# Block-sparse attention and a gated feed-forward layer on one core: the loads of the second batch lose their gate, one early key load goes to another queue, and the order of all engines is written anew

## The chip, the core and the metric

The kernel runs on one core of one Trainium2 chip. The core has five engines with a queue of instructions each: TensorE (PE in the profile, its weight loads PEld) multiplies matrices, VectorE (DVE) and ScalarE (ACT) work element by element, GpSimd (POOL) does so too and issues some transfers, and SyncE (SP) only issues transfers. Each engine takes its instructions in the order in which they are written; between engines semaphores make one wait for another. Transfers run on 16 DMA engines. The metric is the device time of one execution in microseconds (us), the median of several runs; less is better.

## The reference

```python
scores = scale * np.matmul(q, k.transpose(0, 1, 3, 2))    # q, k, v: 4 batches, 8 heads, 768 positions, 64
mask = |blk_i - blk_j| <= 1, first and last block row and column, 3 sampled blocks per row   # blocks of 32
attn = softmax(np.where(mask, scores, -1e9))
x = np.matmul(attn, v) -> (3072, 512)                     # heads side by side
h = x @ w_in                                              # 512 x 2048
out = (h * (1.0 / (1.0 + np.exp(-beta * h)))) @ w_out     # 2048 x 512, float32
```

Inputs and output are float32. The kernel computes in float16 with float32 sums.

## The kernel before

**Attention.** Two heads are handled together as a pair, 4 pairs a batch, 16 in all. For each pair the keys, queries and values are loaded (tile `st`, or a part of the still unused tile `g`, called `es` in the program), cast to float16 (`s` for keys and queries, `va` for values) and, for keys and queries, transposed so that the head's 64 numbers lie on the partitions (`kX`, `qX`, four sets). For batch 0 PE transposes; for batches 1 to 3 SP issues a transposing DMA. A unit is one pair with 256 or 512 queries; there are 32 units. In a unit PE writes blocks of scores into PSUM (`sc`), ACT takes the exponential of each block of 128x1024 (`et`), DVE multiplies it with a mask of zeros and ones (`mask01`), PE multiplies it with the values, DVE divides by the row sums (`recip`, `xst`), and the result is transposed into `x`: by PE for batch 0 and by a DMA on SP later. The first four units are masked on PE instead, by an additional matmul with `shut_qk`.

**Feed-forward.** The 3072 tokens go in seven tiles (256, five of 512, 256). For each tile there are 16 blocks of `x @ w_in` (the program's kind `hp`), the tanh of it on ACT (`th`, tile `t_sb`), the product on DVE (`gm`, tile `g`), and the product with `w_out`: plain for the first tile (`op`), and for the other six with seven half-size products instead of eight (`pr`), for which DVE forms sums and differences of `g` and, once, of `w_out` (`w_mix`).

**Masks.** `add_mask` makes the mask at the start: DVE finds the sampled blocks, PE spreads them over the partitions, one copy makes `mask_q`, PE spreads that three times (`km`), and three copies from PSUM fill `mask01` (`kmc`); one more instruction makes `shut_qk`. In the table of before ACT makes `mask_q` and `shut_qk`, and DVE makes all three copies to `mask01`. beta is loaded by ACT's queue (`emit_first`), transposed by PE and copied by DVE; the tanh needs it.

**Order.** Everything is made as a list of nodes, numbered in the order of `add`. The table `STEPS` sets the order: `92A0` is node 92 on ACT with buffer 0, `86P2:85` is two nodes of PE of which the matmuls are split in two halves of 64 rows and sent alternately. The program is emitted in the table's order, so each engine's queue is the table read for that engine. When a pair of nodes is sent in halves, GpSimd's queue gets an empty instruction that waits for the end of both (`one.met`), so GpSimd's queue also passes PE's pairs in the table's order. `dur` and `at` in the nodes were used when the table was made, and set nothing when it runs.

**Loads.** All loads of keys, queries and values are issued by SP, in the table's order. The weights are issued by GpSimd, in three parts for `w_in` (4, 4 and 8 of 16 blocks) and three for `w_out`; they start when the load `q3` has landed (`GATE`; GpSimd writes one number of `w_in_sb` from the landed tile first). For the first pair of batch 1 the key, query and value loads have a gate of their own (`gate` in `add_load`): GpSimd copies one number of `w_out_sb` into the staging tile, which can only be done when that part of `w_out` has landed (part 0 for keys and queries, part 8 for values), and the load, which overwrites the tile, has to wait for the copy. SP takes its rows in order, so the loads behind wait too.

Of the kernel before, what the change touches and what calls it, by code (L numbers as in the profile page):

```python
# [43 lines left out]
30S0 31G2 32P5 12S3 0D 1P1 13D0 14P4 10P6 33A1 2A 34S1 35G3 38S 11D 15D0 3A 36P0 39D 4P2 37D 6P3  # L44
16S4 20S 24S 21G 7D 17D3 44S0 40P7 41D 64S4 48S1 91P2 92A0 95P0 96A3 65G6 22P3 18P6 58S3 25D 5D
23D 19D 93P2 94A1 81P0 82A9 45D3 46P2 79P3 26P4 49D3 54S2 27D 50P3 80A2 83P2 84A4 28S4 42S5 72G
73G 74G 29G0 47D2 51D 105P0 52S6 107P3 55D4 59D1 56P2 60P3 57D3 61D 106A5 103P0 108A6 104A7
86P2:85 117P3 118A8 62S7 85P 115P1 119P0 43G1 87D0 88D4 66P4 97P3 98P 75G 116Aa 53G2 67D 63G3 99Dg
100D0 89P2 190P2 120Ab 8P3 193P3 187P0 9D 90D0 191Ac 76G 77G 109P2 110P 68S8 194Ad 199P1 69D0 70P6
101P7 188A0 111Df 112D1 121P2:122 71D 211P0 78G 200A1 122P 102D 123D2 124D2 212Ae 214P1 196P3  # L50
113P4 125P5 220P0 201D 126D 114D 215A6 221A8 216D 195D 222D 127P3 128A1 145P2 136P1 197A2 146A2
148P0 137A0 202P3 139P45:142 142P 192D 203A3 149A5 129D0 147D 138D 198D 189D 143A3 140A4 217P1
150D 130P1 157P7 154P6 144D 141D 213D 204D 218A9 158A4 159D 131A6 155A1 132D 172P0 173A2 174D
133P2 134A0 235G8 151P5 152A5 163P7 166P4 164A4 226P0 167A3 156D 135D 153D 168D 223P1 165D 227A4
169P6 160P4 170A3 219D 161A1 171D 228D 162D 205P0:206 252P3 206P 246P2 224A5 253A7 247Aa 225D
249P1 230P3:229 250Ab 236S 207Dc 208D0 261P0 290P2 291A3 239G5 229P 248D 254D 251D 231De 232D4
292D 175P23:181 258P2 237D2 262A0 243G1 240S 241G6 259A1 181P 278P0 255P3 263D 279A2 256Ac 238S1
182P 176P 287P2 280D 288A8 183P:177 281P0 293P3 244S 270S5 271G5 260D 362D 257D 358D 359D 360D
294A9 177P 284P2 285Ae 282Ad 289D 295D 283D 286D 184P 178P 179A1 185A0 242S 264P2:265 414P3 415A4
405P0 265P 399P1 406A5 273S3 276S2 400A6 272S2 296P3 297P 209P0 266D2 363D 267D1 268P1 233P4 402P1  # L60
210A2 269A 274G1 302S8 305S7 407D 298De 299D2 300P0 403A9 275S 234D 301D 308S6 422S4 408P3 411P2
412A0 310P0 322P2 311A0 323A6 313P1 331P3 314A2 409A8 332A5 401D 404D 364D 365D 312D1 361D 303G4
319P4 320A4 277D1 306G2 245G0 324D 316P0 304S0 317A3 315D 333D 328P2 329A1 430P3 343P13:325 431A7
321D 436P2 325P 437Ad 425S0 428S5 433P3 318D 330D 416D 413D 410D 423G0 438D 326A0 344A5 327D 345D
426G3 337P5 334P4 434Ac 352P2 439P3 338A2 335A4 340P1 366D0 339D 353A0 432D 354D 336D 440A3 424S3
346P0 341A5 307S 445P1 347A6 349P76:355 446Ae 442P2 355P 443A1 342D 348D 441D 447D 435D 418P1:417
444D 453P0 350A6 356A1 417P 454Aa 456P2 459P0 429G3 309G2 419D2 420D0 427S 186S 457A8 448P1:449
460Ab 465P2 466A5 357D 351D 369D 180S 449P 468P3 469A3 462P0 463A6 375P4 488P3 367D 450D4 451D1
455D 482P1 372P5:376 489A0 476P0 376P 483A2 485P3 477A4 479P1 373P 467D 461D 458D 464D 470D 471P0
370D 484D 486Ad 480A9 472P 374D0 377D 473D2 474D3 586P1 587A5 491P3 383P:380 583P0 594P1 608S1  # L70
611S3 492A7 609G6 478D 487D 490D 493D 368D 584A8 481D 371D 379D 378D 380P 381P:384 580P0 619P3
384P 595Ac 382D 620Ae 495P1:494 622P3 494P 581A1 385A1 616P0 623Aa 614S2 630S8 421S1 631G1 612G5
389P 600P3 496D7 497D4 641P1 386P:390 617Ad 601Ab 638P0 642A3 621D 585D 633S6 636S0 652S5 653G4
655S7 475S 610S1 452S 498S 644P3 390P 582D 588D 658S4 639A6 597P1 387P 598A0 645A2 391D 640D 388D
624D 602D 499P0 500A5 517P1 656G2 518A6 501D0 519D 505P4 506A3 507D 589P1 590P 613S 660P3 674S1
392P0:508 661A4 596D 591Df 634D0 502P14:514 663P3 632S2 508P 675D6 592D2 646D 599D 514P 666P1
664A7 509A6 511P6 510D 515A5 516D 665D 643D 503A3 667A9 512A1 538P0 654S3 677S3 526P4 393P 527A4
539A2 394A 678G3 513D 504D 615G0 635S 682P1 688P3 689A1 520P1 529P5 521A3 683A5 530A0 618D 528D
662D 540D 625P3 626P 535P4 657S 676S0 593S2 679S 680S8 397S 398S 522D 627Db 628D0 637D2 531D 668D
536A6 699P0 696P1 603P3 604P 700A8 605D7 606D2 544P5 697Aa 545A3 523P0 537D 701D 547D0 546D 524A5  # L80
684D 525D 659G1 685P3 710P1 532P1 711Ac 647P2 541P2 533A2 534D 648P 649D5 650D1 686Ad 669P0:670
702P3 542A5 703Ae 543D 670P 808P2 671D5 672D3 704D 550D 690D 698D 687D 551D 548D 553P23:556 716P3
814P0 556P 557P:554 809A6 815A0 820P2 717Ab 713P0 554P 821A2 805P3 555D1 558D 691P2 692P 693D3
561P 714A3 806A4 817P3 818A7 694D4 828P0 706P2:705 851S5 854S3 857S2 607S 829A9 564P:562 552D 715D
560D 831P3 705P 707D5 708D2 562P 859P2 832A1 681G3 629S 396S 882S4 885S0 811P3 865P0 695S 395S
651S 888S7 712D 718D 860A5 549D 565P 563A 812A8 566A0 673S 709S 866Ad 719P2 720P 567P 568P 861D
559D 721D2 819D 722D0 816D 723S 862P3 840P2 843P0 841A3 863Ae 844Aa 807D 822D 883G6 569D 570P 571P
855G1 572D 864D 810D 813D 573P 724P4 725A6 727P1 748P3 728A1 852D5 749A0 837P3 838Ab 726D1 729D
750D 845D 824P2:823 834P0 823P 871P3 757P3:574 835Ac 868P0 872A4 574P 825Dh 890P3 869A0 758A1
891A8 913S6 916S1 884S1 826D4 842D 867D 839D 575D 759D 733P54:730 874P0 730P 875A2 739P23:745  # L90
896P3 893P0 734A5 731A0 836D 873D 833D 735D 830D 897A6 853S2 919S8 886G0 745P 746A2 740A4 732D
741D 894A7 760P5 742P4 876D 917G4 914G3 769P7 743A4 744D 770A6 771D 736P2 846P0 847P 899P3 761A3
577S 856S 762D 763P54:751 737A0 848Db 849D2 747D 900A1 738D 902P0 751P 903A3 764A0 752A5 1002P3
1005P0 772D0 901D 765D 870D 1006Ac 753D 766P2 767A6 754P3 1025S4 755A2 1003Aa 768D 877P0 878P 887S
915S3 578S 905P2 756D 906Ab 879D9 880D3 1014P1 1015A9 778P67:781 1008P0 827S1 920G2 895D 907D 892D
775D 904D 898D 776D 773D 1011P2 918S 579S 576S 1028S8 1012A0 781P 782P:779 1009A4 1056P1 1036P2
1057A2 1031S3 779P 780A1 783D 908P0:909 1045P1 909P 889G0 1037Ae 1046Ad 786P:789 1048P2 1039P1
1040A5 910Da 911D1 784D 1049A1 789P 790P:787 1032D3 1026D1 850S 881S 912S 1033P0 1017P1 787P
# [30 lines left out]
SHUT = 30000.0  # L129
CUTS_IN = (0, 4, 8, 16)  # L130
CUTS_OUT = (0, 4, 8, 16)
GATE = "q3"
EARLY = ("k2", "q2", "k3", "q3", "v0", "v1", "v2", "v3", "r1")
SLACK = 1500
X_SLACK = 1500
# [96 lines left out]
def kernel(  # L232
# [11 lines left out]
    nc = tc.nc  # L244
# [4 lines left out]
    P = 128  # L249
# [823 lines left out]
```

## Time and profile before

| | |
|---|---|
| median of 3 runs | 263.57 us (262.94 to 264.21) |
| the profiled execution's own time | 264.08 us |
| its span | 262.3 us |
| PE, DVE, ACT, POOL busy | 251.7, 229.1, 210.2, 40.3 us |
| granted PE clock | 1.0 throughout |
| read from HBM, written | 27.27 MB, 6.29 MB |

The span runs from the first to the last recorded instruction; the time is 1.8 us longer. Nearly all instructions have the line of a helper that records them (L198), so groups are told apart by tiles: `et<-sc` on ACT is an exponential, `sc<-va,et` on PE is the product with the values, `sc<-x,w_in_sb` an `hp`. "issue" as the end of a wait means that the engine waited for nothing that the profile shows. The queue q1 holds the transfers that SP and ACT issue, q0 those of GpSimd, and q8 the instructions that the engines' sequencers fetch.

### The profile page before, as it was taken

The numbers are of one execution on the slowest core, as the hardware profiler recorded it, in microseconds if no ns is written. First come the engines' busy times: TensorE is split into PE (matmuls) and PEld (weight loads), VectorE is DVE, ScalarE is ACT, GpSimd is POOL, SyncE is SP. The second block draws the span as 40 slices with busy tenths as digits, with TensorE's granted clock in tenths as the row PEclk, the third lists the DMA queues.
The fourth block names the chain that finished last, engine by engine and source line by source line (L and its number), as shares of the span: only waits on it lengthen the run. The fifth ranks groups of instructions, "written<-read, shape, count | busy, mean of one in ns | idle before, by whom it ended". The sixth has DMA issues, their size and how long they took to land.

```text
span 262.3 us, 8817 instructions
## 1 busy us (share of the span) xinstructions
PE 251.7 (96%) x3767; PEld 171.3 (65%) x3767; DVE 229.1 (87%) x446; ACT 210.2 (80%) x282; POOL 40.3 (15%) x58
## 2 busy tenths in 40 slices
PE   6998999999969998999999999999999999999995
PEld 2684664554447876558876457856757996468884
DVE  4566999999979999899899989999989897799692
ACT  4799999999979995999888989886899792764421
POOL 4273003114220141201021121130000000000000
PEclk9999999999999999999999999999999999999999
DMA  5999994988797359699246945650050202300042
GB/s 161 332 309 212 206 210 99 289 222 170 181 293 243 60 108 200 132 280 222 65 94 167 204 97 139 162 83 0 2 179 6 42 4 95 99 2 0 2 159 81
DMA packets 50154, 36.81 MB, mean 140 GB/s; under 512 B 29748, under 2 KB 46660, under 8 KB 50116
## 3 DMA queue, kind: packets, MB, share of 16 engines
q1 hardware_dynamic: 46368, 32.06, 48.4%
q0 software_dynamic: 3680, 4.19, 9.3%
q8 instruction: 29, 0.48, 0.8%
q14 instruction: 9, 0.07, 0.1%
q10 hardware_dynamic: 68, 0.01, 0.0%
HBM read 27.27 MB, written 6.29 MB: 128 GB/s over the span
## 4 chain that ended last, share of the span: by engine, by line
PE 78%; ACT 8%; DVE 6%; DMA 3%; issue 3%; SPq 0%; POOL 0%; DVEq 0%; POOLq 0%; ACTq 0%
PE sc L198 78%; ACT et L198 4%; ACT t_sb L198 3%; DMA qX<-s 2%; DVE et L198 2%; DVE g L198 2%; DMA st<-in_q_dram 1%; DVE xst L198 1%; SPq L503 0%; DVE kX L198 0%; DVE s L198 0%; DVE osb L198 0%; DVE qX L198 0%; DVE recip L198 0%; DVE x L198 0%
## 5 line engine op out<-in xcount | busy, mean ns | idle before, releaser
L198 ACT ACTIVATE et<-sc 128x1024 f16<-128x1024 f32 x144 | 139.9, 1037 | 16.8 <-PE sc L198 13.8
L198 PE MATMUL sc<-x,w_in_sb 128*128 128x512 f16 (+3 forms) x512 | 92.8, 350 | 0.5 <-ACT et L198 0.2
L198 DVE TENSOR_TENSOR et<-et,mask 128x960 f16<-128x960 f16 x132 | 85.1, 684 | 1.0 <-ACT et L198 0.9
L198 ACT ACTIVATE t_sb<-sc,beta_c_sb 128x512 f16<-128x512 f32 (+1 forms) x112 | 65.3, 644 | 23.9 <-PE sc L198 17.2
L198 DVE SCALAR_TENSOR_TENSOR g<-t_sb,sc 128x512 f16<-128x512 f16 (+1 forms) x112 | 63.7, 606 | 6.1 <-ACT t_sb L198 5.5
L198 PEld LDWEIGHTS <-w_in_sb 128*128 128x128 f16 (+1 forms) x512 | 42.9, 97 | 37.5 <-issue 3.6
L198 PEld LDWEIGHTS <-g 64*128 64x128 f16 (+1 forms) x692 | 49.3, 96 | 14.1 <-issue 3.8
L198 PE MATMUL sc<-w_out_sb,g 64*128 64x256 f16 (+3 forms) x560 | 55.7, 280 | 0.1
L198 PE MATMUL sc<-qX,kX 64*128 64x512 f16 (+1 forms) x384 | 52.0, 330 | 2.2 <-DMA qX<-s 0.8
L198 PEld LDWEIGHTS <-et 64*128 64x128 f16 (+1 forms) x1776 | 41.6, 95 | 11.4 <-issue 3.6
L198 PE MATMUL sc<-va,et 64*128 64x65 f16 (+1 forms) x1776 | 45.1, 191 | 2.3 <-issue 1.5
L198 POOL CAST s<-st 128x768 f16<-128x768 f32 (+2 forms) x23 | 19.5, 859 | 72.9 <-DVE et L198 24.6
L198 PEld LDWEIGHTS <-kX 64*128 64x128 f16 x384 | 19.4, 96 | 13.6 <-issue 8.8
L198 PEld LDWEIGHTS <-s 64*128 64x128 f16 (+1 forms) x320 | 21.8, 97 | 7.1 <-issue 2.3
L198 PE MATMUL sc<-w_mix,s 64*128 64x256 f16 (+1 forms) x272 | 24.0, 270 | 0.0
L198 DVE TENSOR_TENSOR xst<-sc,recip 128x256 f16<-128x256 f32 (+1 forms) x32 | 17.8, 556 | 0.9
L198 PE MATMUL sc<-w_mix,g 64*128 64x256 f16 (+3 forms) x128 | 15.4, 264 | 0.0
L198 DVE TENSOR_TENSOR osb<-osb,sc 128x512 f32<-128x512 f32 (+2 forms) x19 | 11.7, 614 | 3.8 <-PE sc L198 3.0
L198 POOL CAST va<-st 128x768 f16<-128x768 f32 x9 | 8.6, 959 | 38.0 <-DVE xst L198 10.9
L198 DVE RECIPROCAL recip<-sc 128x4 f32<-128x4 f32 (+1 forms) x32 | 6.2, 193 | 9.4 <-PE sc L198 9.1
L198 ACT COPY osb<-sc 128x512 f32<-128x512 f32 (+3 forms) x18 | 9.4, 530 | 5.9 <-PE sc L198 4.4
L198 DVE TENSOR_TENSOR g<-g 128x1024 f16<-128x1024 f16 (+1 forms) x12 | 8.1, 690 | 0.0
(59 smaller groups left out, 95.2 us busy)
## 6 DMA issues: line engine op xcount, KB each, us to landing
out_dram<-osb SPq DMA_DIRECT2D x23, 256.0 KB, 2.5
st<-in_k_dram SPq DMA_DIRECT2D x12, 384.0 KB, 4.7
st<-in_q_dram SPq DMA_DIRECT2D x12, 384.0 KB, 4.2
st<-in_v_dram SPq DMA_DIRECT2D x12, 384.0 KB, 4.8
g<-in_v_dram SPq DMA_DIRECT2D x4, 384.0 KB, 7.8
w_in_sb<-in_moe_w_in_dram POOLq DMA_DIRECT2D x2, 512.0 KB, 10.3
w_in_sb<-in_moe_w_in_dram POOLq DMA_DIRECT2D x1, 1024.0 KB, 12.1
w_out_sb<-in_moe_w_out_dram POOLq DMA_DIRECT2D x2, 512.0 KB, 13.2
```

The lines of the kernel that those rows point to most:

```text
L198: r = f(*a, **kw)
```

## The change

Four things change. The gates of the first pair of batch 1 are gone: `add_prep(y)` is called without `gates`, so three one-number copies on GpSimd and what they wait for are left out; in the dependencies of batch 1's loads only their order behind the earlier loads is left. One early key load (`BESIDE`: keys of pair 1, from chunk 2 on, two of heads x 256 numbers in a row) is issued by ACT's queue, in the place where ACT issued the load of beta; the load of beta becomes a node on SP. The copies of the mask may be placed on GpSimd as well. And the table `STEPS` is another one. In the new table all four copies of the mask (nodes 3, 5, 7 and 9: `3A`, `5A`, `9A`, `7A`) stand on ACT and none on GpSimd; DVE, which made three of them, makes none.

```diff
-30S0 31G2 32P5 12S3 0D 1P1 13D0 14P4 10P6 33A1 2A 34S1 35G3 38S 11D 15D0 3A 36P0 39D 4P2 37D 6P3
+0D 1P0 3A 4P7 8P6 2A 5A 9A 35S4 31S0 32D0 36D1 39S 40D 41P5 49S1 65S4 13S1 33P6 37P1 34A2 42D 6P5
...
+BESIDE = ("k", 1, 2)
+COPY384 = {"ACT": 395, "DVE": 465, "POOL": 480}
...
     def copy_on(eng):
-        return act.copy if eng == "ACT" else dve.tensor_copy
+        return {"ACT": act.copy, "DVE": dve.tensor_copy, "POOL": pool.tensor_copy}[eng]
...
         nc.scalar.dma_start(out=sb_i32, in_=sb_lo)
-        nc.scalar.dma_start(out=beta_sb, in_=moe_beta.rearrange("(c p) -> c p", p=P))
+        for load in beside:
+            load()
...
-        n_mtc = add("mask", ("ACT", "DVE"), {"ACT": 395, "DVE": 465}, 100, mtc, deps=[n_mt], use=[tb])
+        n_mtc = add("mask", ("ACT", "DVE", "POOL"), COPY384, 100, mtc, deps=[n_mt], use=[tb])
...
+        def load_beta():
+            nc.sync.dma_start(out=beta_sb, in_=moe_beta.rearrange("(c p) -> c p", p=P))
+        n_lb = add("load", "SP", 560, 0, load_beta, moved=8192)
+        n_bt = add("beta", "PE", 120, 200, bt, deps=[n_lb], take=[bb])
...
         src = {"k": k, "q": q, "v": v}[nm]
+        other = (nm, x, lo) == BESIDE
...
-            nc.sync.dma_start(out=at(st)[:, :, lo * D:hi * D], in_=rows[:, :, lo * D:hi * D])
+            (nc.scalar if other else nc.sync).dma_start(out=at(st)[:, :, lo * D:hi * D], in_=rows[:, :, lo * D:hi * D])
         early = x < NPAIR
-        deps = [] if early else [(d, -1e9) for d in last_load + begin]
+        deps = [] if early else [(d, -1e9) for d in last_load + (begin if x >= 2 * NPAIR else [])]
...
+        if other:
+            beside.append(load)
+            kw["at"] = 1410.0
+
+            def load():
+                pass
...
-                    add_prep(y, (0, 0, 8) if y == NPAIR else (None, None, None))
+                    add_prep(y)
```

Three places of the order follow. In them `st`, `s`, `va`, `kX`, `qX`, `sc`, `et`, `xst` and `x` carry the number of the buffer.

**ACT's queue at the start**, first before, then now. `sb_i` holds the sampled blocks; `onehot`, `mask_q`, `shut_qk` and `mask` belong to the mask; `et` is the first exponentials.

```order
L360 DMA sb_i_158<-in_sampled_blocks_dram 24x6
L361 DMA beta_sb<-in_moe_beta_dram 16x128
L389 ACT_TABLE_LOAD
L389 COPY onehot<-g_111 128x384
L198 COPY kX_124<-sc_63 128x256
L198 ACTIVATE shut_qk<-sc_61 128x128
L198 CAST mask_q<-sc_61 24x384
L198 ACTIVATE et_65<-sc_63 128x1024
L198 ACTIVATE et_68<-sc_61 128x1024
```

```order
L362 DMA sb_i_158<-in_sampled_blocks_dram 24x6
L510 DMA st_130<-in_k_dram 128x2x256
L392 ACT_TABLE_LOAD
L392 COPY onehot<-g_111 128x384
L200 CAST mask_q<-sc_61 24x384
L200 ACTIVATE shut_qk<-sc_61 128x128
L200 CAST mask_157<-sc_64 128x384 x2
L200 COPY kX_126<-sc_64 128x256
L200 CAST mask_157<-sc_63 128x384
L200 ACTIVATE et_79<-sc_62 128x1024
L200 ACTIVATE et_65<-sc_64 128x1024
```

Three mask copies now stand ahead of the first exponential, the key load has beta's place, and of the first two score blocks, which PE writes to `sc_64` and then to `sc_62`, ACT now takes the second one first.

**GpSimd's queue around the weights**, first before, then now. The `L509` rows are the gate copies; a cast `s<-st` or `va<-st` serves batch 1.

```order
L198 CAST va_120<-g_111 128x12x64
L198 CAST va_121<-g_111 128x12x64
L480 DMA w_out_sb<-in_moe_w_out_dram 128x4x512 x2
L480 DMA w_out_sb<-in_moe_w_out_dram 128x8x512
L509 CAST st_138<-w_out_sb 1x1
L509 CAST st_135<-w_out_sb 1x1
L509 CAST st_131<-w_out_sb 1x1
L198 CAST s_6_145<-st_135 128x2x6x64
L198 CAST s_5_144<-st_135 128x2x6x64
```

```order
L483 DMA w_in_sb<-in_moe_w_in_dram 128x4x512
L200 CAST va_118<-g_111 128x12x64
L483 DMA w_in_sb<-in_moe_w_in_dram 128x4x512
L483 DMA w_in_sb<-in_moe_w_in_dram 128x4x1024
L200 CAST s_6_145<-g_111 128x2x4x64
L486 DMA w_out_sb<-in_moe_w_out_dram 128x4x512 x2
L486 DMA w_out_sb<-in_moe_w_out_dram 128x8x512
L200 CAST s_3_142<-st_132 128x2x6x64
L200 CAST s_1_140<-st_137 128x2x6x64
```

The gate copies are gone, so SP's first loads of batch 1 no longer stand behind `w_out`; the second part of `w_in` now stands behind a cast of values, and `w_out` behind a cast of the last query load of batch 0.

**SP's queue where batch 1's transposes end and batch 2's loads begin**, first before, then now. `out_dram<-osb` are the stores of the first feed-forward tile; `x<-xst` carries a finished attention unit into `x` and waits for DVE.

```order
L549 DMA_TRANSPOSE kX_128<-s_0_139 128x6x128
L549 DMA_TRANSPOSE qX_123<-s_2_141 128x6x128
L549 DMA_TRANSPOSE qX_129<-s_3_142 128x6x128
L834 DMA out_dram<-osb_112 128x512
L834 DMA out_dram<-osb_113 128x512
L503 DMA st_131<-in_k_dram 128x2x384
L503 DMA st_133<-in_q_dram 128x2x384
L503 DMA st_132<-in_v_dram 128x2x384
L503 DMA st_138<-in_k_dram 128x2x384
L725 DMA_TRANSPOSE x_115<-xst_80 128x4x128
L503 DMA st_136<-in_q_dram 128x2x384
L503 DMA st_130<-in_v_dram 128x2x384
```

```order
L847 DMA out_dram<-osb_113 128x512
L562 DMA_TRANSPOSE kX_128<-s_2_141 128x6x128
L562 DMA_TRANSPOSE qX_129<-s_0_139 128x6x128
L847 DMA out_dram<-osb_112 128x512
L510 DMA st_137<-in_k_dram 128x2x384
L510 DMA st_132<-in_q_dram 128x2x384
L510 DMA st_136<-in_v_dram 128x2x384
L738 DMA_TRANSPOSE x_114<-xst_83 128x4x128
L738 DMA_TRANSPOSE x_114<-xst_82 128x4x128
L510 DMA st_138<-in_k_dram 128x2x384
L510 DMA st_135<-in_q_dram 128x2x384
L510 DMA st_133<-in_v_dram 128x2x384
```

Before, four loads stand in a row, one transpose behind them, and four more loads behind that; now three loads stand in a row, and the next three stand behind two transposes, each of which waits for a finished unit.

167 lines of the change are left out of this document (83 added, 84 removed).

## The prediction

> **What bounds the kernel now.** I read the engines' busy time first, then the same by stage, then the chain that ended last, and last PE's own waits. Busy time:
>
> ```profile
> PE 251.7 (96%) x3767; PEld 171.3 (65%) x3767; DVE 229.1 (87%) x446; ACT 210.2 (80%) x282; POOL 40.3 (15%) x58
> ```
>
> By stage (two stretches that read alike are left out):
>
> ```profile
> core 0: us, PE busy (x) PEld busy (x) DVE busy (x) ACT busy (x) POOL busy (x), PEclk, DMA share, GB/s
> 8.00:20.00 12.00, 11.56 (x197) 8.51 (x194) 7.17 (x18) 11.32 (x12) 6.69 (x10) 1.00 1.08 320
> 20.00:41.00 21.00, 19.41 (x384) 13.08 (x384) 18.46 (x45) 20.61 (x34) 3.35 (x5) 1.00 1.07 194
> ...
> 76.30:77.80 1.50, 0.00 (x0) 0.00 (x0) 0.64 (x2) 0.55 (x1) 0.00 (x0) 1.00 1.68 328
> 77.80:101.64 23.84, 22.77 (x415) 17.44 (x415) 23.08 (x38) 21.18 (x24) 4.74 (x5) 1.00 0.64 133
> 101.64:258.94 157.30, 157.17 (x2233) 112.36 (x2234) 141.60 (x264) 119.63 (x164) 11.87 (x13) 1.00 0.40 100
> ```
>
> From 101.64 us on PE is busy for 157.17 of 157.30 us: only less PE work helps there, and the change has as many matmuls as before. Whatever is won or lost lies ahead of 101.64 us, and from there it goes to the end undiminished. From 20 to 41 us ACT is full (20.61 of 21.00), and in one stretch of 1.5 us PE stops altogether. The end of the early part in the chain of waits, and PE's waits:
>
> ```profile
> 95.56 5.95 DMA qX<-s
> 101.51 0.14 issue
> 101.64 64.67 PE sc L198 x914
> ```
>
> ```profile
> PE sc L198 <- issue: 1.7, 2, 1.5
> ...
> PE sc L198 <- DMA qX<-s: 0.8, 1, 0.8
> ```
>
> No row of PE's waits names the gates or a load of batch 1. The two waits that this change can reach are the 1.5 us of "issue" and the 0.8 us for a transposed query tile.
>
> **The hole at 76.3 us.** PE's timeline there:
>
> ```profile
> 75.52 0.77 PE L198 MATMUL sc<-va,et 64*128 64x65 f16 x37
> 77.80 0.35 PE L198 MATMUL sc<-va,et 64*128 64x65 f16 x11 [1.51 <-issue]
> ```
>
> PE stops inside one group of 48 matmuls, after 37, waiting for no semaphore. I take it for a late instruction fetch. The fetches of the whole page; the only data queue's row for 61.5 to 75.4 us, where no fetch stands; both queues' rows for 75.4 to 78 us; and PE's work in the first of these stretches:
>
> ```profile
> q8 instruction: 29, 0.48, 0.8%
> ```
>
> ```profile
> q1 hardware_dynamic: 4582, 2.94, 90.8%
> ```
>
> ```profile
> q1 hardware_dynamic: 912, 0.81, 148.3%
> q8 instruction: 1, 0.02, 2.2%
> ```
>
> ```profile
> 61.40:75.40 14.00, 13.44 (x218) 6.41 (x216) 13.68 (x24) 13.88 (x20) 4.37 (x5) 1.00 0.91 211
> ```
>
> 29 packets for 3767 + 3767 PE instructions are one for every 260. In this stretch PE took 218 + 216 = 434 without one. What filled the DMA engines was SP's row of loads:
>
> ```profile
> 71.25 0.44 SPq L503 DMA_DIRECT2D st<-in_k_dram  x1
> 71.74 0.51 SPq L503 DMA_DIRECT2D st<-in_q_dram  x1
> 72.35 0.48 SPq L503 DMA_DIRECT2D st<-in_v_dram  x1
> 72.87 0.47 SPq L503 DMA_DIRECT2D st<-in_k_dram  x1
> ```
>
> Four loads of 384 KB are 1.57 MB; at the 320 GB/s of the first stage that is 4.9 us of backlog, just where the products with the values (a weight load and a matmul for 65 columns) use up instructions fastest.
>
> **The change, part by part.**
>
> *Gates.* Three copies leave GpSimd, and with them SP's waits:
>
> ```profile
> L509 POOL CAST st<-w_out_sb 1x1 f32<-1x1 f16 x3 | 1.8, 585 | 15.5 <-PE sc L198 8.6 <-DMA w_out_sb<-in_moe_w_out_dram 7.0
> ```
>
> ```profile
> SPq L503 <- POOL st L509: 28.5, 2, 21.8
> ```
>
> Directly this is worth 0: PE never waited for these loads. Indirectly SP's row moves forward, by at most the 28.5 us. Less is left at the stores and at batch 2's loads, since transposes of batch 1 stand in between that need a set which batch 0 still reads and casts behind its last values; I reckon with some 5 us. Then batch 2's first three loads go near 66 us, under feed-forward matmuls that need few instructions, and the three behind them wait for two `xst` of units whose products are the very ones around the hole. The backlog at 72 to 76 us is gone, and with it the 1.5 us. Bounds: 0 (a fetch is late all the same, there or elsewhere) to -1.5. I take -1.5: the hole needs loads and products with values at the same time, and the new row parts them.
>
> *The wait for the query tile.* SP's timeline behind the `qX` that is issued at 95.56 us, and the usual time to landing:
>
> ```profile
> 96.83 0.57 SPq L503 DMA_DIRECT2D st<-in_k_dram  x1
> 97.51 3.52 SPq L549 DMA_TRANSPOSE kX<-s  x2
> ```
>
> ```profile
> qX<-s SPq DMA_TRANSPOSE x12, 2.8
> ```
>
> It took 5.95 us instead of 2.8; a load and two transposes went right behind it. In the new row a store that waits for the feed-forward stands between. And on PE one product group (8 matmuls of 256 columns; 32 such take 4.12 us in a row below, so about 1.0) is put ahead of the scores that waited. Bounds -0.8 to 0; either covers it: -0.8. DVE, nearly full there (23.08 of 23.84), also has two of that stretch's three casts ahead of it now.
>
> *The weights pay.* In the DMA engines the key and query load of batch 1 (0.77 MB) now stand right behind batch 0's loads, and `q3`, which starts the weights, has 384 KB more ahead of it, since `q2` moved to the front. GpSimd's issue of the last part of `w_in`, its time to landing, the weights' queue from 16 to 38 us, and PE's group that first uses this part:
>
> ```profile
> 17.50 0.74 POOL L477 DMA_DIRECT2D w_in_sb<-in_moe_w_in_dram  x1
> ```
>
> ```profile
> w_in_sb<-in_moe_w_in_dram POOLq DMA_DIRECT2D x1, 1024.0 KB, 12.1
> ```
>
> ```profile
> q0 software_dynamic: 3584, 4.11, 109.0%
> ```
>
> ```profile
> 30.08 4.12 PE L198 MATMUL sc<-x,w_in_sb 128*128 128x256 f16 x32
> ```
>
> At 320 GB/s the two are 2.4 and 1.2 us, 3.6 together. The part landed at 17.50 + 12.1 = 29.6 us; by the table the second block of the group at 30.08 uses it, at 30.5: 0.9 us of slack. The new table uses it about 1 us later (one exponential more stands ahead of the first tanh). So the wait is between 0 and 3.6 - 1.9 = 1.7 us. GpSimd issues some parts behind casts now, yet q0 always had work (109% of 16 engines), so a later issue alone costs 0. I take +0.4, nearer to 0, because the two queues share the engines and the new loads will not all go first.
>
> *The start.* ACT's timeline, DVE's mask copies, and the issues that move:
>
> ```profile
> 4.70 0.45 ACT L198 CAST mask_q<-sc 24x384 f16<-24x384 f32 x1
> 7.96 1.94 ACT L198 ACTIVATE et<-sc 128x1024 f16<-128x1024 f32 x2 [2.81 <-PE sc L198]
> ```
>
> ```profile
> L198 DVE CAST mask<-sc x3: 551/558/558, 6.5 to 20.8; 128x384 f16<-128x384 f32 x3
> ```
>
> ```profile
> 1.75 0.46 SPq L503 DMA_DIRECT2D st<-in_q_dram  x1
> 2.26 0.47 SPq L503 DMA_DIRECT2D st<-in_k_dram  x1
> ```
>
> ```profile
> 1.42 0.33 ACTq L361 DMA_DIRECT2D beta_sb<-in_moe_beta_dram  x1
> ```
>
> Three mask copies at 0.45 are 1.4 us, under ACT's wait of 2.81: 0 (and 1.4 if that wait were gone). DVE is rid of three at 0.56, mostly in its slack (7.17 of 12.00): 0. The first query load goes two issues of SP earlier (2 x 0.51 = 1.0), the key load 2.26 - 1.42 = 0.8. Against it ACT takes the second score block first: about +0.85, since PE's two blocks are one exponential (1.94 / 2 = 0.97) or a little less apart. Together about 0, bounds -1.0 to +1.0; I take 0, as a full ACT must still do all exponentials of batch 0. beta is needed by the first tanh only, long after: 0. The Trainium skill ("Trainium Kernel Development and Optimization", Key Constraints) says that issuing from several engines saves the sequencer's issue time alone; by that the second queue is worth one SP issue and the start comes out no better than 0.
>
> *GpSimd and the mask.* In the new table no mask copy is on GpSimd, so that part of the change does nothing. Five casts move from GpSimd to DVE; at the 0.56 of the mask copies, that is 2.8 against the 1.7 it loses: +1.1 us, where it idles 4.8 us (before 20 us) and 15.7 us (behind 101.64): 0, and 1.1 if that cover were gone.
>
> *The tail.* ACT's last copy was followed by a small DVE addition and the store; now the small block is multiplied earlier and ACT's copy is last.
>
> ```profile
> 259.31 0.22 DVE L198 TENSOR_TENSOR osb<-osb,sc 128x64 f32<-128x64 f32 x1 [0.69 <-ACT osb L198]
> ```
>
> The addition leaves the end (-0.2), but its matmuls, which ran under ACT's copy, now run ahead of it (+0.2): 0.
>
> Sum: -1.5 - 0.8 + 0.4 = -1.9 against the execution's own 264.08 (span 262.3), so 262.2; it was 0.5 above the median of 263.57, and the terms are differences: against the median **261.7 us**.
>
> **The rivals.** A measurement of this kernel tells 0.5%, 1.3 us, from no change: 262.25 to 264.89 is "the same".
>
> B, *the hole stays*: three loads do as four did, or the loads were not the cause. For it: the products with values stand as densely as before. Against it: the one hole lies in the densest DMA (148.3%). -0.8 + 0.4: 263.2. The Trainium skill speaks for it: "DMA: Bandwidth & Descriptors" (Queues, rings and completion order) lets a DMA engine take turns between its queues packet by packet, so that a backlog in one would hardly hold up another; no row here can show the turns.
>
> C, *the weights are late in full* (+1.7) while the hole goes: -1.5 - 0.8 + 1.7: 263.0. For it: ACT is full from 20 to 41 us, what it waits there is lost. Against it: the table uses them later.
>
> D, *slower: batch 1's early loads hold up weights and fetches in the first 41 us.* For it: the engines are at 1.08 and 1.07 there already. Its price: 1.7 for `w_in`, 1.5 for a new hole of the kind above, with both old waits left: 263.57 + 3.2 = 266.8. It decides when the last part of `w_in` lands behind 31.5 us. Against it: 0.77 MB are a fifth of the 4.11 that the weights move.
>
> **How the numbers follow.** Forecast 0.5 (its own range 260.5 to 262.9), B 0.25, C 0.1, D 0.15. The range goes from 260.0 (the start's -1.0 and 0.7 for smaller waits) to 265.2, which holds B, C and the smaller half of D. Faster: 0.5 x 0.8 + 0.25 x 0.15 + 0.1 x 0.2 = 0.46; slower: D and a little of B, 0.17; within 0.5%: the rest, 0.37.
>
> **What would show it.** Right, if PE's waits have no "issue" above 1 us, the row of PE's wait for `qX<-s` is gone, and the stretch in which PE never idles begins about 2 us before 101.64. Wrong, if PE or ACT waits for `w_in_sb` between 26 and 33 us, if the first exponential starts after 8.9 us, or if the hole is there again. If PE's busy time in the last stretch differs by more than 1 us, I looked at the wrong part of the kernel.

## The result and the profile after

The changed kernel takes 262.39 us (median of 20 runs, 261.58 to 263.5) against 263.88 for the kernel before (20 runs beside it): ratio 0.9929, 95% interval 0.9908 to 0.9950, so 1.5 us faster by the medians, a gain of less than one per cent that both intervals keep clear of zero. In a later comparison the same two kernels gave 0.9960 (0.9940 to 0.9980). The profiled execution of the changed kernel took 262.88 us, 1.2 less than the 264.08 of the one before. In 6 of 24 other executions of the kernel before the mean granted clock was 0.991 to 0.994 and the time 264.7 to 266.2 us, while in none of the changed kernel's 20 was the clock below 0.998.

Busy time of the engines after, and four of the stretches by which the prediction read the kernel before:

```profile
PE 249.6 (96%) x3767; PEld 171.8 (66%) x3767; DVE 226.2 (87%) x445; ACT 213.7 (82%) x288; POOL 34.8 (13%) x50
```

```profile
8.00:20.00 12.00, 11.38 (x204) 8.75 (x200) 5.89 (x15) 10.46 (x13) 5.92 (x10) 1.00 1.08 341
20.00:41.00 21.00, 18.32 (x349) 13.22 (x347) 17.74 (x44) 20.94 (x33) 3.77 (x6) 1.00 1.13 187
76.30:77.80 1.50, 1.50 (x74) 1.08 (x66) 1.50 (x3) 1.50 (x2) 0.14 (x1) 1.00 0.70 236
101.00:257.90 156.90, 156.27 (x2198) 111.12 (x2198) 141.68 (x264) 121.33 (x166) 10.36 (x10) 1.00 0.42 99
```

PE works through the 1.5 us in which it stood still before, and the last stretch is nearly as full as it was (0.63 us without PE work, 0.13 before). The waits of PE after:

```profile
PE sc L200 <- ACT et L200: 1.5, 4, 0.5
PE sc L200 <- DVE g L200: 1.3, 2, 0.8
PE sc L200 <- DVE xst L200: 1.2, 4, 0.3
```

The long "issue" is gone, and the wait for `qX<-s` but for 0.13 us. New are the waits for VectorE's `g` and `xst`, of at most 0.8 us each; all but one of 0.49 us (at 106.75) lie ahead of 57 us, in the part that loses time.

Three landmarks tell where the time went; at each PE has the same work behind it (some products are cut into halves in one order and whole in the other), and at the first ScalarE has one exponential more behind it. First before, then after: tile 1's first feed-forward products, the first product group with `w_out` of that tile, and PE's last work.

```profile
55.58 6.22 PE L198 MATMUL sc<-x,w_in_sb 128*128 128x512 f16 x28
...
78.51 1.05 PE L198 MATMUL sc<-w_out_sb,g 128*128 128x256 f16 x8
...
258.10 1.05 PE L198 MATMUL sc<-w_mix,g 128*128 128x192 f16 x16
```

```profile
56.77 5.56 PE L200 MATMUL sc<-x,w_in_sb 128*128 128x512 f16 x25
...
78.12 1.03 PE L200 MATMUL sc<-w_out_sb,g 128*128 128x256 f16 x8
...
257.10 0.82 PE L200 MATMUL sc<-w_mix,g 128*128 128x192 f16 x8
```

Up to tile 1 the change **loses** 1.19 us (55.58 to 56.77). Between the first two landmarks it wins 1.58 (from +1.19 to -0.39): the stop of 1.51 us is in there. From 78 us to PE's end it wins another 0.84 (-0.39 to 257.92 - 259.15 = -1.23). So the profile's sum is +1.2 - 1.6 - 0.8, and the loss at the start is the part that the prediction took as 0. A second execution of each kernel gives +1.14, -1.82 and -0.71 by the same landmarks.

### The profile page after: what moved, and what is told of

Same layout as the page of the kernel before. It is cut to its first block, busy times and chain, and to the rows that moved or that the text cites. A ratio compares the mean times of both kernels' runs of the same rounds, so it can differ in the third digit from the quotient of the medians.

```text
span 261.1 us, 8802 instructions
## 1 busy us (share of the span) xinstructions
PE 249.6 (96%) x3767; PEld 171.8 (66%) x3767; DVE 226.2 (87%) x445; ACT 213.7 (82%) x288; POOL 34.8 (13%) x50
## 4 chain that ended last, share of the span: by engine, by line
PE 83%; DVE 11%; DMA 1%; ACT 1%; issue 1%; POOL 1%; SPq 0%; DVEq 0%; ACTq 0%
PE sc L200 83%; DVE et L200 5%; DVE g L200 3%; DMA st<-in_k_dram 1%; DVE xst L200 1%; ACT et L200 1%; DVE s L200 1%; DVE recip L200 0%; POOL s L200 0%; POOL va L200 0%; DVE kX L200 0%; ACT t_sb L200 0%; DVE va L200 0%; DVE x L200 0%; SPq L510 0%
## 5 line engine op out<-in xcount | busy, mean ns | idle before, releaser
L200 PE MATMUL sc<-x,w_in_sb 128*128 128x512 f16 (+2 forms) x504 | 92.1, 352 | 1.1 <-ACT et L200 0.5
L200 DVE TENSOR_TENSOR et<-et,mask 128x960 f16<-128x960 f16 x132 | 83.2, 670 | 1.4 <-ACT et L200 1.2
L200 PE MATMUL sc<-qX,kX 64*128 64x256 f16 (+1 forms) x384 | 50.6, 328 | 1.4 <-DVE g L200 0.8
L200 PE MATMUL sc<-va,et 64*128 64x65 f16 (+1 forms) x1776 | 44.3, 191 | 0.8 <-DVE xst L200 0.3
L200 POOL CAST s<-st 128x768 f16<-128x768 f32 (+2 forms) x17 | 15.1, 905 | 87.4 <-PE sc L200 34.5
L200 POOL CAST va<-st 128x768 f16<-128x768 f32 x10 | 9.6, 968 | 59.0 <-DVE g L200 32.0
L200 ACT COPY osb<-sc 128x512 f32<-128x512 f32 (+3 forms) x19 | 10.0, 539 | 8.5 <-PE sc L200 7.5
L200 DVE CAST s<-st 128x768 f16<-128x768 f32 (+2 forms) x15 | 7.7, 522 | 2.0 <-DMA st<-in_k_dram 2.0
```

The lines of the kernel that those rows point to most:

```text
L200: r = f(*a, **kw)
```

## The experiments

Ratios are to the kernel before, timed beside each.

**The kernel before, a second execution** (no edit).

> The kernel before, unchanged, looked at in a second execution. If the stop of TensorE belongs to the order of the work (a late instruction fetch behind four loads in a row), the trace has it again: an idle time of 1.3 to 1.7 us with no releaser ('issue') between 75 and 79 us, inside a group of products with the values. If it was an accident of the one execution that the prediction read, there is no idle time over 1 us of that kind, and the span is 1 to 1.5 us shorter than 262.3. The wait of 0.8 us for a transposed query tile near 101 us is asked in the same way.

The stop is there again, and in the same place: PE's timeline there.

```profile
75.85 0.77 PE L198 MATMUL sc<-va,et 64*128 64x65 f16 x37
78.38 0.35 PE L198 MATMUL sc<-va,et 64*128 64x65 f16 x11 [1.76 <-issue]
```

It again stops after 37 of the 48 products. The wait for `qX<-s` was 0.5 us this time, not 0.8. The stop near 77 us belongs to the kernel, not to one execution. PE's waits have a second stop, though:

```profile
PE sc L198 <- issue: 3.1, 2, 1.8
```

The other 1.33 us of the 3.1 end at 41.41 us, after 607 matmuls and 608 weight loads. The first execution had no such stop there, so this one comes and goes.

**Two of the four loads moved** (kernel before, SyncE's row):

```diff
 st<-in_k_dram
 st<-in_q_dram
-st<-in_v_dram
-st<-in_k_dram
 x<-xst (transpose)
+st<-in_v_dram
+st<-in_k_dram
```

> The kernel before with one edit: of the four loads that SyncE issues in a row at 71.25 to 72.87 us, the last two (a value and a key load of batch 2) go behind the next transpose of x (issued at 74.44). Gates, start and every other engine stay. If the stop of TensorE comes from the loads that clog the DMA engines, it is gone or below 0.5 us and the time falls by about 1.5 us, to 262.4 (ratio 0.994). Rival: the stop is not the loads' doing, it stays at 1.5 us and the time is the same within 0.3 us (263.9, ratio 1.000). If the stop goes and the time stays, the 1.5 us were cover for another wait.

The profiled execution has the stop unchanged, although only two loads stand ahead of it now. SyncE's and PE's timelines:

```profile
70.97 1.00 SPq L834 DMA_DIRECT2D out_dram<-osb  x2
72.03 0.43 SPq L503 DMA_DIRECT2D st<-in_k_dram  x1
72.51 0.50 SPq L503 DMA_DIRECT2D st<-in_q_dram  x1
75.22 1.20 SPq L725 DMA_TRANSPOSE x<-xst  x1
```

```profile
78.82 0.35 PE L198 MATMUL sc<-va,et 64*128 64x65 f16 x11 [1.76 <-issue]
```

Timed, it is 263.12 against 263.61 (0.9964, 0.9935 to 0.9993): some gain in other executions, a third of what was expected. "Four loads in a row" was thus not the cause as the prediction put it. What stood out instead was the place: always the same instruction. Counting PE's matmuls and weight loads up to the stop, in the kernel before and up to the small stop of the changed kernel at 39.36 us:

```profile
0.00:77.70 77.70, 71.50 (x1118) 41.36 (x1119) 64.20 (x144) 69.03 (x93) 23.71 (x40) 1.00 0.95 225
```

```profile
0.00:39.30 39.30, 33.14 (x479) 22.48 (x479) 26.15 (x76) 33.73 (x50) 11.89 (x27) 1.00 1.06 244
```

1118 + 1119 = 2237 and 479 + 479 = 958: 1279 apart, which is 5 x 256 less 1. The fetches are 16 KB each, and 29 of them for 7534 instructions: a fetch is a block of about 256. Smaller stops fit this: one of 0.22 us in the kernel before stands at instruction 447 (20.03 us), the one of its second execution at 1215. All these counts lie within two of 191 + 256 n, and 7534 instructions have 29 such places, as many as there are fetches. So every stop without a releaser stands at a block's edge; that it comes from a late fetch is what the next experiments ask.

**All four loads moved** (kernel before; the transpose of `x` goes ahead of all four).

> The kernel before with all four loads of 71.25 to 72.87 us put behind the next transpose of x; nothing else moves. Theory, after the spread of two loads left the stop in place: TensorE's instructions come in blocks of 256 (the stop sits at its instruction 2237 in every run of the old order, and the changed kernel's small one of 0.15 us at 39.36 us at instruction 958, 1279 = 5 x 256 - 1 apart); TensorE goes on 1.3 to 1.5 us after the block's fetch has landed, and the fetch waits until what SyncE issued before it has drained. With two stores and two loads ahead that was 76.5 us; with the two stores alone it should start by about 74, land by 75, and let TensorE go on at 76.3, when it gets there: the stop below 0.3 us, the time 1.0 to 1.5 us lower (262.3, ratio 0.995), unless the next fetch is late by about 0.5 us behind the moved loads. Rival: the stop stays at 1.5 us whatever the loads do, ratio 1.000.

The stop is gone, as the theory has it: PE runs through the group of 48.

```profile
76.24 0.93 PE L198 MATMUL sc<-va,et 64*128 64x65 f16 x48
```

But the time falls by 0.7 us only (263.28 against 263.94; 0.9977, 0.9952 to 1.0001), which is not clear of zero. A new wait took the rest of the gain; PE's waits have it at the top:

```profile
PE sc L198 <- DMA x<-xst: 1.9, 1, 1.9
```

A cast of keys behind the moved loads starts at 91.22 us instead of 86.79 and keeps a transpose of keys and then the last transposes of `x` back (93.34 us instead of 90.26); tile 2's first products wait for these. It is not the load that holds the cast (it landed at 79.81 us). The edit moved this cast in the table too, so that in GpSimd's row it stands behind two more of PE's pairs (their empty instructions end at 87.83 and 89.87 us), and then it waits for VectorE until 91.13. GpSimd's timeline:

```profile
91.22 2.79 POOL L198 CAST s<-st 128x768 f16<-128x768 f32 x3 [15.54 <-PE sc L198]
```

So the 1.9 us are a side effect of this edit on GpSimd, and not the price of later loads.

**Four loads in a row in the changed kernel** (two loads of batch 2 moved up):

```diff
 st<-in_k_dram
 st<-in_q_dram
+st<-in_k_dram
+st<-in_q_dram
 st<-in_v_dram
 x<-xst (transpose) x2
-st<-in_k_dram
-st<-in_q_dram
```

> The changed kernel with one edit on SyncE: two loads of batch 2 (a key and a query load, 384 KB each) are issued right behind the two at 70.3 and 70.8 us, so that four stand in a row as in the kernel before. If the backlog of loads makes the fetch late, the fetch that starts at 74.12 us in the changed kernel starts some 2.4 us later (0.77 MB at 320 GB/s), at about 76.5, TensorE stops for 1 to 2.3 us near 77 to 79 us, and the time rises by as much: 263.4 to 264.6 (ratio 0.998 to 1.003). Rival: fetches are served beside the loads, no stop over 0.4 us, time as the changed kernel's 262.4 (0.994).

The stop comes back in a kernel that had none there, after 13 of 48 products now, since the order is another; the count up to it is 2236 again. The timeline, and the count:

```profile
76.46 0.39 PE L200 MATMUL sc<-va,et 64*128 64x65 f16 x13
78.43 0.74 PE L200 MATMUL sc<-va,et 64*128 64x65 f16 x35 [1.58 <-issue]
```

```profile
0.00:78.40 78.40, 70.11 (x1118) 42.32 (x1118) 61.88 (x139) 71.16 (x97) 22.68 (x38) 1.00 0.93 229
```

The time is 264.34, 1.9 us above the changed kernel's 262.4 (ratio 1.0018, 0.9986 to 1.0050). With the experiment before, this shows it both ways: what SyncE has issued when a block's fetch comes due makes PE stop. The fetch packets of the traces agree with PE's next instruction (us); "edge before" is when PE passed the block's edge ahead of the one in question:

```
run                            edge before  fetch starts  landed  PE goes on  after landing
kernel before                     72.68        75.42       76.36     77.80        1.44
kernel before, 2nd execution      73.01        75.95       76.96     78.38        1.42
two loads moved                   73.45        76.52       77.42     78.82        1.40
gates removed alone               73.24        76.30       77.51     78.88        1.37
four in a row, changed kernel     72.73        75.93       76.84     78.43        1.59
all four moved                    73.41        74.28       75.16   (no stop)
changed kernel                    72.99        74.12       75.30   (no stop)
changed kernel, at 39 us          34.49        36.94       37.98     39.36        1.38
```

PE goes on 1.4 to 1.6 us after the fetch has landed. In the run with two loads moved the fetch starts at 76.52, 1.4 us after the last of the two stores and two loads ahead of it could be done at 320 GB/s (1.3 MB from 71 us on are 4.1 us, to 75.1); in the changed kernel one store and two loads are ahead, and it starts at 74.12. From the edge before, the fetch takes 2.7 to 3.2 us to start in the five runs with the stop near 77 us, and 0.9 and 1.1 in the two without. This does not grow with the backlog: two stores and four loads (2.1 MB) gave 2.7 to 3.1 us, one store and four loads (1.8 MB) 3.2, two stores and two loads (1.3 MB) 3.1, but one store and two loads (1.05 MB) 1.1. How the fetch is queued behind them these traces do not show.

**The three gates removed alone** (kernel before; every row but GpSimd's gates and the loads behind them as it was).

> The kernel before without its three gate copies; the order on every engine is otherwise that of before, row for row. By the prediction the gates are worth 0 directly, the stop at 76 us goes (SyncE's loads are no longer in one row there) for -1.5 us, and the weights wait 0 to 1.7 us behind the two early loads of batch 1: 262.4 to 264.1 (ratio 0.994 to 1.001), TensorE or ScalarE waiting for w_in near 30 us where the weights are late. Rival: the gates do nothing at all here; the same time (1.000) with the stop still there.

It is no gain, and not clearly a loss: 264.51 against 263.61 (1.0024, 0.9990 to 1.0058). PE's waits:

```profile
PE sc L198 <- issue: 2.3, 2, 2.0
...
PE sc L198 <- DMA w_in_sb<-in_moe_w_in_dram: 1.1, 1, 1.1
```

The last part of `w_in` lands at 31.51 us instead of 29.65, and the first product that needs it waits 1.10 us. The stop did not go: SyncE's row there begins with transposes of batch 1 that wait for that batch's own casts (its four loads start at 71.82 us, against 71.25 before), so loads that are 20 us earlier in batch 1 do not bring those of batch 2 forward. Behind the stop of 2.03 us the granted clock is one half, in the stretch from 78.88 to 82.24 us:

```profile
78.88:82.24 3.36, 3.36 (x25) 1.58 (x26) 2.80 (x6) 1.94 (x2) 0.00 (x0) 0.50 0.67 201
```

Half the clock for 3.36 us is 1.7 us of work, and this execution, with 266.18 us, lies 1.7 above the median of its twelve. The stops of 1.5 to 1.8 us and the wait of 1.94 us in the other traces had full clock behind them.

**The gates put back into the changed kernel** (GpSimd, behind the last issue of the weights):

```diff
 w_out_sb<-in_moe_w_out_dram (last part)
+st<-w_out_sb  (gate, keys)
+st<-w_out_sb  (gate, queries)
 s<-st         (cast, keys of batch 1)
+st<-w_out_sb  (gate, values)
```

> The changed kernel with the three gate copies put back on GpSimd behind the last issue of the weights, and SyncE's first loads of batch 1 waiting for them; all else in the order of the change. In the old order the gates' removal made TensorE wait 1.1 us for w_in and the time 0.6 us longer. In the new order nothing waits for w_in, so theory: the gates bring the weights in earlier by up to 2.4 us (0.77 MB at 320 GB/s), which nobody waits for, and the time is the same within 0.3 us (262.4, ratio 0.994). Rival 1: the late batch 1 loads hold TensorE up near 45 us, 0.5 us or more slower. Rival 2: the fetch at 36.94 us comes earlier with the weights out of its way, and the time falls by 0.2 to 0.5 us.

Rival 1 holds in place and sign, and its size is far larger than any that was expected: 269.76 us, 1.0225 (1.0193 to 1.0258), 7.3 us above the changed kernel. GpSimd's gates ran at 40.11 us, SyncE's loads followed, and VectorE, where the cast of these queries stands at 39.9 us in the new order, waited in front of it:

```profile
40.11 0.30 POOL L516 CAST st<-w_out_sb 1x1 f32<-1x1 f16 x2 [16.52 <-PE sc L200]
```

```profile
45.31 0.56 DVE L200 CAST s<-st 128x768 f16<-128x768 f32 x1 [5.50 <-DMA st<-in_q_dram]
```

PE waits behind VectorE, and then goes on at half the clock; its longest wait, and the stretch that follows it:

```profile
PE sc L200 <- DVE g L200: 6.4, 3, 5.1
```

```profile
46.26:50.79 4.53, 4.53 (x22) 1.72 (x23) 3.41 (x7) 3.27 (x4) 1.38 (x2) 0.50 0.41 76
```

The wait of 5.06 us and half of 4.53 are the 7.3 us. So the new order rests on the early loads of batch 1: VectorE's first cast for that batch stands at 39.91 us, against 42.44 in the old order. This is the price at one place of the gates in GpSimd's row; others were not tried.

**The early key load back on SyncE** (`BESIDE = None`).

> The changed kernel with the early key load (the second part of batch 0's second key tensor) issued by SyncE in its place in SyncE's row instead of by ScalarE; nothing else moves. Theory: the 1.2 us by which tile 1 starts later in the changed kernel do not come from this load; the load on ScalarE's queue shares the DMA engines with the first key part (issued at 1.26 us it landed at 5.09, against 4.05 for the second load of the kernel before), so on SyncE the first part lands earlier, the second a little later, and the first exponential moves by less than 0.5 us: time the same within 0.3 us (262.4, ratio 0.994). Rival 1: the second queue is what wins here; without it the first exponential is 0.5 us or more later and the time 0.5 us higher (0.996). Rival 2: it costs, and the time falls by 0.5 us or more (0.992).

262.34 us, 0.9939 (0.9918 to 0.9960): the same. The first exponential starts at 9.53 us instead of 9.46. The second queue is worth nothing here that these runs can tell.

**The mask copies back on VectorE** (changed kernel):

```diff
-5A 9A
+5D 9D
...
-7A
+7D
```

> The changed kernel with the three mask copies that went to ScalarE (0.45 us each, all ahead of 8.2 us) back on VectorE, the order otherwise kept. By the prediction they cost nothing on either engine: the first exponential within 0.5 us of 9.46 us, the time the same within 0.3 us (262.4, ratio 0.994). Rival: VectorE, which casts the first keys and queries at 5.1 us and copies kX and qX at 6.6 to 7.4, gets 1.7 us of copies in front of these, the first exponential is 1 us or more later, and 0.3 to 1 us of it reaches the end (0.995 to 0.998).

The rival holds, and more: 264.87 us (1.0054, 1.0032 to 1.0076), 2.4 above the changed kernel beside it (262.45). VectorE's and ScalarE's timelines:

```profile
4.88 1.02 DVE L200 CAST mask<-sc 128x384 f16<-128x384 f32 x2 [1.62 <-PE sc L200]
5.82 0.82 DVE L200 CAST s<-st 128x256 f16<-128x256 f32 x3
```

```profile
10.85 1.94 ACT L200 ACTIVATE et<-sc 128x1024 f16<-128x1024 f32 x2 [2.93 <-PE sc L200]
```

Two mask copies, 1.02 us together, push the first casts from 5.12 to 5.82 us, the third pushes `qX` from 7.08 to 8.81, and the first exponential starts 1.4 us later than in the first execution of the changed kernel (9.46 us). On ScalarE the same copies fill waits. The profiled executions differ by 1.5 us (264.36 against 262.88); the rest of the 2.4 is in no trace here.

**The first exponential's scores first** (changed kernel, PE):

```diff
-96P3 94P1 95Ae
+94P1 96P3 95Ae
```

> The changed kernel with two TensorE steps exchanged: the scores that the first exponential reads are computed ahead of the other score block, as in the kernel before. In the changed kernel the first exponential starts at 9.46 us instead of 7.96, and tile 1's feed-forward starts 1.2 us later than before. If the order of the two blocks is 0.85 of that and the early part passes it on, the first exponential starts at about 8.6 us and the time is 0.85 us below the changed kernel's 262.4 (261.5, ratio to before 0.991). Rival: the 20 to 41 us stretch is held by something else (TensorE's products, w_in), the exponential is earlier and the time stays 262.4 (0.994).

ScalarE starts 1.0 us earlier, and nothing of it reaches the end: 262.37 us (0.9919, 0.9880 to 0.9958). The interval alone holds the expected 0.85 us as well as 0; the trace tells them apart. ScalarE's and PE's timelines:

```profile
8.45 1.94 ACT L200 ACTIVATE et<-sc 128x1024 f16<-128x1024 f32 x2 [0.49 <-PE sc L200]
11.15 0.37 ACT L200 COPY kX<-sc 128x256 f16<-128x256 f16 x1 [0.76 <-DVE kX L200]
```

```profile
39.38 0.77 PE L200 MATMUL sc<-va,et 64*128 64x65 f16 x38 [0.41 <-issue]
```

Three quarters are gone at 11 us, in a wait for VectorE's copy of `kX`; the other quarter goes at the block's edge at 39 us, where the stop grows from 0.15 to 0.41 us and PE goes on at 39.38 instead of 39.36. Here the late fetch swallowed what was left of the gain.

**The changed kernel, a second execution** (no edit).

> The changed kernel itself, timed beside the others on the same chip and looked at a second time: ratio 0.991 to 0.995, no wait of TensorE over 1 us without a releaser, a small stop of 0.1 to 0.5 us near 39 us at its instruction 958.

262.45 against 263.37 (0.9960, 0.9940 to 0.9980). Everything at the start is 0.5 us earlier than in the first execution (first exponential at 8.98 us). The stop at 39 us is 0.90 us instead of 0.15, above the 0.5 that was expected, and PE goes on 0.28 us later than in the first execution:

```profile
39.64 0.77 PE L200 MATMUL sc<-va,et 64*128 64x65 f16 x38 [0.90 <-issue]
```

**Only SyncE's row changed** (kernel before, gates and start as they were):

```diff
+out_dram<-osb x2
 kX<-s (near 57 us)
...
-out_dram<-osb x2
 st<-in_k_dram
 st<-in_q_dram
+x<-xst (transpose)
 st<-in_v_dram
 st<-in_k_dram
-x<-xst (transpose)
...
-st<-in_v_dram
 qX<-s (near 95 us)
-st<-in_k_dram
 kX<-s
+st<-in_v_dram
+st<-in_k_dram
```

> The kernel before with SyncE's row alone changed, gates and all else kept: the two stores of 70.2 us go in front of a key transpose near 57 us (their data are ready at 51), of the four loads behind them the last two go behind the next transpose of x, and near 95 us a value and a key load go behind the next key transpose instead of around the query transpose that TensorE waited for. Theory: with the stores and two loads gone from the backlog the fetch that is due at 72.7 us starts by 73.5 and the stop of 1.5 us is gone; the wait of 0.3 to 0.8 us for the query tile is gone too, and no wait for a transposed x takes their place as it did with all four loads moved (1.9 us). Time 1.8 to 2.3 us below before (261.6 to 262.1, ratio 0.992), so at or 0.5 us below the changed kernel, with the gates in place. Rival: the transposes of x are late again and the gain is 0.7 us, as with the four loads moved (0.9975).

262.24 us against 263.37 (0.9943, 0.9921 to 0.9965); the changed kernel beside it had 262.45. The wait for the query tile is gone, the stop nearly, and no wait for `x` came. SyncE's and PE's timelines:

```profile
69.63 0.58 SPq L503 DMA_DIRECT2D st<-in_k_dram  x1
70.25 0.47 SPq L503 DMA_DIRECT2D st<-in_q_dram  x1
73.91 1.20 SPq L725 DMA_TRANSPOSE x<-xst  x1
```

```profile
75.97 0.35 PE L198 MATMUL sc<-va,et 64*128 64x65 f16 x11 [0.22 <-issue]
```

The fetch starts at 73.45 us and the stop shrinks to 0.22. The profiled execution gained 2.5 us (261.57), the medians 1.1: as much as the whole change, or 0.2 more, which the intervals do not separate. No version was shown to beat the change.

**The same without the gates.**

> The kernel with the new row of SyncE (before with two stores and four loads moved, 262.24 us, ratio 0.994) without its three gate copies; every other row on every engine the same. In the old row the gates' removal came together with a longer stop (2.0 instead of 1.5 us) and a wait of 1.1 us for the last part of w_in. Theory: the wait for w_in is what the early loads of batch 1 cost the weights, it comes back here at 0.8 to 1.5 us with the stop still below 0.5 us, and the time rises by 0.5 to 1.5 us over the same kernel with gates (262.7 to 263.7, ratio to before 0.996 to 1.000). Rival: in a row without the backlog the gates are free to go, no wait for w_in over 0.3 us and the time stays at 262.2 (0.994).

262.89 us (0.9970, 0.9944 to 0.9995), 0.65 above the same kernel with gates, in another comparison, with intervals that overlap. In the profiled execution PE's matmuls did not wait for `w_in` (a weight load did, for 0.2 us): the last part landed at 31.11 us, 3 us later than with gates (28.14), but the group of PE whose second block needs it began at 30.60 us, against 29.84 in the old order without gates. Whether the weights are late depends on how the start falls out; what the gates are worth in the old order lies between 0 and some 0.9 us and stays open.

## Why the prediction was right, and where it was not

Time and sign are right: 261.7 us were forecast, 262.39 measured, a gain of 1.9 against 1.5 by the medians. The sum has one term missing (a loss of 1.2 at the start) and one too many (0.4 for the weights); that these two partly cancel is luck.

- **The hole, -1.5: right in size and in kind** (-1.58 between the landmarks). The stop is a late fetch, made late by what is queued in the DMA engines: taking the loads away removed it, putting two back in the changed kernel made it again. The details were wrong. Four loads are not what it takes: with two stores and two loads ahead the stop was whole (1.76 us). And the path was another: batch 2's first loads do not go near 66 us; they go at 70.31 and 70.79 us, and the value load behind them waits to 75.69. What parts the backlog from the due fetch is that one of the two stores and two of the four loads no longer stand right ahead of it. SyncE's timeline after:

```profile
69.73 0.53 SPq L847 DMA_DIRECT2D out_dram<-osb  x1
70.31 0.43 SPq L510 DMA_DIRECT2D st<-in_k_dram  x1
70.79 0.49 SPq L510 DMA_DIRECT2D st<-in_q_dram  x1
75.69 0.37 SPq L510 DMA_DIRECT2D st<-in_v_dram  x1
```

  Nor is it the gates' removal that does it, as the working had it: without gates and with the old rows the stop was 2.0 us. The new order does it. Rival B (the hole stays, three loads doing as four) did not come true, but it was near: two stores and two loads were enough for the stop. The rule that it cited, the Trainium skill's "DMA: Bandwidth & Descriptors" (Queues, rings and completion order), has each DMA engine take turns between its queues. The fetch nevertheless started 1.8 and 2.4 us later with a larger backlog (75.93 and 76.52 against 74.12), so here the measurement speaks against a fetch that simply passes the backlog; whether it is held in the DMA engines or asked for later, no trace shows.
- **The wait for the query tile, -0.8: right**, 0.13 us of the wait are left, and the stretch behind 78 us gains 0.84 (0.71 in the second executions). In the other runs with the old order near 95 us the wait was 0.3 to 0.5, so 0.8 was one execution's number.
- **The weights, +0.4: nothing in the new order, mechanism right.** The last part of `w_in` lands at 30.71 us instead of 29.65 and PE never waits for it, since the new order uses it later; in the old start the same removal cost PE 1.10 us once and next to nothing another time, inside the bounds of 0 to 1.7.
- **The start, 0 with bounds of 1.0: wrong.** The text named a first exponential after 8.9 us as a sign against it; it came at 9.46 and 8.98. Tile 1 starts 1.19 us later; in five traces with the old start it begins between 55.05 and 56.35 us, in three with the new one between 56.52 and 57.05, so the size varies and the sign does not. Of the first exponential's 1.5 us the order of the two score blocks is 1.0 (0.85 was reckoned), and the gain of q and k (1.0 and 0.84) did not come: the query tile landed early, at 3.00 us, but the first key part, now issued behind it at 1.26 us, took 3.83 us and landed at 5.09, and VectorE's three casts stand behind it. The chain of waits and VectorE's timeline after:

```profile
1.26 3.83 DMA st<-in_k_dram
```

```profile
5.12 0.83 DVE L200 CAST s<-st 128x256 f16<-128x256 f32 x3 [1.86 <-DMA st<-in_k_dram]
```

  In the second execution the first key part landed at 3.80 us, and the third cast waited for the other part, ScalarE's load, which landed at 5.02; the exponential came at 8.98 all the same. VectorE's timeline there:

```profile
5.04 0.43 DVE L200 CAST s<-st 128x512 f16<-128x512 f32 x1 [0.72 <-DMA st<-in_k_dram]
```

  Giving the 1.0 back did not bring the time back, so the 1.2 us have more than one cause: VectorE's copies at 11 us and the block's edge at 39 us each hold the work back in these traces. That ScalarE's one more exponential ahead of the first tanh does so too is not shown. Which of them is worth most stays open.
- **The mask copies, 0 on either engine: half right.** On ScalarE they fill waits; that they cost nothing on VectorE was read from the old start, and no run tested it there. In the new one VectorE's early casts are what ScalarE waits for, and the three copies are worth 2.4 us by the medians. ScalarE also took three copies (`kX`, `x`, `osb`) from VectorE that the prediction did not count: it has 288 instructions instead of 282.
- **The gates, directly 0: not told from 0 in the old order (up to 0.9 us), wrong for the new**, which breaks without their removal (+7.3 us). A part of a change that is worth nothing alone can be what the rest stands on.
- **The key load on ScalarE, 0: right** (262.34 without it).
- **The tail, 0: right**: from PE's end to the end of the span it is 3.2 us in both. The casts that go from GpSimd to VectorE, taken as 0, were not tested alone.

Forecast for forecast: -1.5, -0.8, +0.4, 0 against -1.6, -0.8, 0, +1.2 in the profiles; that the medians show 1.5 and not 1.2 is within what single executions differ.

## What to carry to other kernels

An idle time with no releaser inside a run of small products can be an instruction fetch: count the instructions up to it, and if it sits at the same count in every run, look at what SyncE issued in the 5 us ahead, and move stores and loads that nobody needs out of there. Six DMA issues moved in this way gave as much as a new order of all engines. A part of a reordered kernel is not priced by its own wait: taking the gates out cost at most 0.9 us in one order and putting them in 7.3 in the other, and mask copies that stood in slack before cost 2.4 us in the new order. And move one engine's row at a time: a cast that moved along on GpSimd took back part of what moving four loads won.

## What the runs showed of the hardware

- PE's instructions arrive in blocks of 256 (stops at 447, 958, 1215, 2236 and 2237 instructions, 29 fetches of 16 KB), and PE goes on 1.2 to 1.7 us after the block's fetch has landed, in every run with a stop. So a fetch that starts late costs its start, about 1.0 us of transfer and 1.4 us more.
- In the kernel before the fetch starts 0.2 to 0.8 us after PE has crossed the edge before at 51.8, 61.4 and 86.1 us, 2.7 us after it at 75.42, and 4.7 in the block behind, where no stop followed; from 110 us on some start ahead of it. Where a block holds many small products (48 products and 48 weight loads in 0.93 us) that is too late: ahead of the stop PE had 3.6 us of work from edge to edge (72.68 to 76.29 us), less than 2.7 + 0.9 + 1.4.
- An idle stretch of PE of 2.03 us was followed by 3.4 us at a granted clock of 0.50, one of 5.06 us by 4.5 us; idle stretches of 1.94 us and less were not. At half the clock these stretches cost another 1.7 and 2.3 us.
- Two executions of one kernel differ by 0.5 us at the first exponential (9.46 and 8.98 us), with the same instructions.
